# New issue order, PSUM banks and copy engines for a one-core attention and gated-MLP block

## The chip, the cores and the metric

The kernel runs on one core of one Trainium2 chip. The metric is device time in microseconds of one execution; the median of several runs is compared. A core has five instruction queues that run side by side: TensorE (PE, matrix products; its weight loads are shown as PEld), VectorE (DVE), ScalarE (ACT), GpSimd (POOL) and SyncE (SP), which here only issues DMAs. Each works its own list in order and waits on semaphores for the others.

## The reference: what is computed

One token block `x` of 2048 tokens by 448 columns goes through two stages, in bfloat16.

Stage A is attention with residual. `x` is normed per token (mean and variance over 448), multiplied by `wqkv` into q, k, v of 16 heads of 28 columns. Each token attends to itself and to seven earlier tokens at distance 2, 4, ... 14 (window 8, dilation 2); positions before the start are masked. The softmax-weighted sum of v is multiplied by `wo` and added to `x`: the result is `h`.

```python
off = jnp.arange(W) * dil            # W, dil = 8, 2
idx = pos[:, None] - off[None, :]
attn = softmax(where(idx >= 0, q . k[idx] * Dh ** -0.5, -1e9))
h = x + (attn . v[idx]) @ wo
z = gelu(layernorm(h) @ w_in)        # 448 -> 1792, z1 and z2 are its halves
g = einsum('ts,sf->tf', w_sp, layernorm(z2)) + b_sp[:, None]
h2 = h + (z1 * g) @ w_out
```

Stage B is a gated MLP. `h` is normed, multiplied by `w_in` (448 by 1792) and put through gelu. The second half of the columns, `z2`, is normed and mixed over all tokens by the 2048 by 2048 matrix `w_sp`; a bias per token is added, the first half `z1` is multiplied in, and `w_out` (896 by 448) brings it back to 448 columns, added to `h`.

## The kernel before

All work is cut into small jobs; each belongs to one engine and holds one or a few instructions. The names below are the job names in the code.

**Attention.** The 2048 tokens are 16 tiles of 128 (`NB`). Per tile m: statistics `st0_m`, mean and variance `mv0_m`, the inverse root `rs0_m` on GpSimd (for tiles 0 and 1 the epsilon is added on VectorE, `ra0_m`), the normed tile `n0_m`. It is transposed to `xhT`: the first four tiles by TensorE with an identity (`xTm`) and copies from PSUM (`xem_i`), the others by a transposing DMA, for which the last 64 columns are copied once more (`nd0_m`). The weights of q and k are padded by four copies `wpc`. Products `qk` (a first group of tokens 0 to 127, a second of 128 to 255 with jobs `qk0F0..2, qk0H, qk1F0..2, qk1H`, then `qk2` to `qk5`) are copied from PSUM by `qe`. The queries of even and odd tokens are handled apart in 17 blocks b (`GEOM`). For each block: two halves of the logits `lgb_0`, `lgb_1` on TensorE (`_0` on row tiles at 0 and 32, `_1` at 64 and 96), their exponentials `exb_0`, `exb_1` on ScalarE, one masking product `mkb` on VectorE, the product with the values and a column of ones `ob`, reciprocal `rcb` and multiplication `omb` on VectorE, the copy of the last columns `odb`, a transposing DMA `oTb`, and a gather `ocb` into `OT`. The values come in pairs of blocks (`vb`, copied by `veb`). For every two tiles, `ym` multiplies by `wo`, `hm` adds the residual on VectorE, and the second layer norm (`st1`, `mv1`, `rs1`, `n1`, `nd1`) ends in a transposing DMA `hTm`.

**MLP.** `z2_m` (16 products, one per tile) and `z1_u` (14 products of two PSUM banks) use `w_in`. Their gelus are on ScalarE (`z2gm`, `z1gu`); where `RAW2` says so, `z2` is first copied raw by `z2cm`. `st2`, `mv2`, `rs2` and `n2_m` norm `z2`. The mixing is cut into 28 tiles of 128 columns by 512 tokens; 13 pairs `gi` and two single ones `g26`, `g27`. Each pair is a list of 64-row products over the 16 tiles of `z2`, first all of kind `a` and then `b`; the first four pairs are cut in eight pieces `gi_0a` to `gi_7a`. VectorE adds the bias (`ua`) and multiplies with `z1` (`um`). `wom` are the output products of two tiles, `wpm_0` (and `_1`) those of the last four tiles one by one; `rm` adds the residual, `outm` stores.

**What sets the order.** Nothing is planned at run time. `Planner.job` lists 886 jobs, and `Planner.order` (line 284) only reads two tables: `ORDER` gives the sequence in which jobs are issued, each to its own engine's list, and `BANKS` the first PSUM bank of each of 147 tickets (a ticket is one or two of the eight banks of 512 columns that a TensorE job fills and another engine empties). `MODE` gives each product its form, in the function `product`. The contraction over 448 rows is three blocks of 128 rows and one of 64:

- `FH`: job `a` does the three blocks of 128 rows for both outputs (six matmuls), job `b` the 64-row rest, two matmuls side by side on the two 64-row tiles of the array.
- `HF`: the same, the rest first.
- `AB`: everything in 64-row halves, eight matmuls in `a` and six in `b`, in pairs side by side.
- `FF` (output products): all 128-row.

`ON` moves single copies to another engine than the default in `move`. Job 885 is a filler: one matmul of 256 columns on constants (line 1078), put where `ORDER` says. The other tables (`KEY`, `WLH`, `LN1G`) do not matter once `ORDER` is fixed.

**What makes a job wait.** `Sched.issue` (line 138) derives the waits from resources that jobs read and write. Each PSUM bank is such a resource (`r_bank`): a TensorE job writes all banks of its ticket, and a job that empties them reads them, so the next TensorE job on a bank waits for the readers of before (lines 1083 to 1094).

## Time and profile before

| what | value |
|---|---|
| runs | 243.03, 242.53, 243.61 us; median 243.03 |
| profiled execution | span 241.8 us, first to last instruction; the profile gives no other time of its own |
| granted TensorE clock, mean | 1.000 |
| instructions | 5654 |
| TensorE busy | 235.9 us, 2431 matmuls |
| VectorE, ScalarE, GpSimd busy | 149.3, 92.0, 40.0 us |
| DMA | 23.20 MB, 96 GB/s in the mean |

The span is shorter than the timed run, which also holds the start and the end of the program. Busy times are sums of durations on an engine. Matmuls overlap in the profile: one is listed with the time until its result is written, so the cost of a group of matmuls is read from its start to the next group's start. A line number such as L462 is that of the helper that issues the matmul of every product, so groups are told apart by the tiles they read (`xhT,wqk` is a `qk` product, `w_in,hnT` is `z1`, `hnT,w_in` is `z2`, `V,E` is `o`, `qkT` the logits, `warm` the filler). Idle time on an engine costs only if TensorE or the end waits for it.

### The profile page before, as it was taken

What the parts mean: (1) busy time and instruction counts of PE and PEld (TensorE: products, weight loads), DVE (VectorE), ACT (ScalarE), POOL (GpSimd) and SP (SyncE); (2) the same over time, 40 slices, a digit from 0 to 9 for tenths busy, and PEclk for the clock granted to TensorE, in tenths of its full rate; (3) what the DMA queues carried; (4) which work ended last, traced back from release to release, by engine and by line L of the source; (5) the groups of instructions that cost most, each with busy time, mean ns of one, the idle gap of its engine ahead of it and who ended that gap; (6) DMA issues with size and microseconds to landing.
All of it is one profiled execution on the core that took longest, in us unless ns stands there. A gap on an engine that the chain in (4) does not pass through costs nothing.

```text
span 241.8 us, 5654 instructions
## 1 busy us (share of the span) xinstructions
PE 235.9 (98%) x2431; PEld 116.3 (48%) x2431; DVE 149.3 (62%) x336; ACT 92.0 (38%) x109; POOL 40.0 (17%) x96
## 2 busy tenths in 40 slices
PE   6999999999999999999999999999999999999995
PEld 4774444554454544444444444444444444444453
DVE  5999988889999999998512306062029031301784
ACT  2478667888889958586802000000000000000000
POOL 6623410101354206235010100000000000000000
PEclk9999999999999999999999999999999999999999
DMA  6963546779698899979999000000000021000022
GB/s 176 308 162 58 115 91 89 158 156 185 129 141 146 129 189 163 221 155 168 191 177 204 3 0 3 0 3 0 0 3 1 0 79 38 0 3 0 3 94 95
DMA packets 66233, 23.20 MB, mean 96 GB/s; under 512 B 58656, under 2 KB 65952, under 8 KB 66208
## 3 DMA queue, kind: packets, MB, share of 16 engines
q1 hardware_dynamic: 66208, 22.83, 47.4%
q8 instruction: 19, 0.31, 0.5%
q14 instruction: 6, 0.05, 0.1%
HBM read 6.72 MB, written 1.84 MB: 35 GB/s over the span
## 4 chain that ended last, share of the span: by engine, by line
PE 88%; DVE 6%; ACT 2%; DMA 2%; issue 0%
PE psum L988 37%; PE psum L462 31%; PE psum L1036 7%; PE psum L1009 3%; PE psum L1078 3%; PE psum L1057 2%; DMA hnT<-xn 2%; PE psum L834 2%; PE psum L810 2%; DVE E L825 2%; ACT E L819 2%; PE psum L705 1%; DVE x_tm L775 1%; DVE st L621 1%; ACT V L505 1%; DVE xn L632 1%
## 5 line engine op out<-in xcount | busy, mean ns | idle before, releaser
L969 DVE TENSOR_TENSOR ub<-psum,bb 128x512 bf16<-128x512 f32 x28 | 18.1, 683 | 52.7 <-PE psum L988 52.7
L988 PE MATMUL psum<-wsp_hi,z2p 64*128 64x512 bf16 x384 | 42.1, 376 | 0.0
L819 ACT ACTIVATE E<-psum 128x960 bf16<-128x960 f32 (+2 forms) x34 | 31.6, 982 | 5.1 <-PE psum L810 4.9
L988 PEld LDWEIGHTS psum<-wsp_hi,z2p 64*128 64x128 bf16 x384 | 18.5, 94 | 23.0 <-issue 0.4
L988 PE MATMUL psum<-wsp_la,z2p 64*128 64x512 bf16 x224 | 26.6, 376 | 0.0
L988 PE MATMUL psum<-wsp_lb,z2p 64*128 64x512 bf16 x224 | 26.4, 376 | 0.0
L899 DVE BATCH_NORM_STATS2 st<-z2p 128x6 f32<-128x448 bf16 x32 | 18.8, 609 | 11.1 <-ACT z2p L895 8.4
L462 PE MATMUL psum<-w_in,hnT 64*128 64x448 bf16 (+1 forms) x206 | 24.9, 350 | 0.6 <-ACT E L819 0.3
L462 PE MATMUL psum<-xhT,wqk 64*128 64x512 bf16 (+3 forms) x206 | 24.4, 351 | 0.0
L462 PE MATMUL psum<-hnT,w_in 64*128 64x512 bf16 (+1 forms) x190 | 23.7, 376 | 0.0
L825 DVE TENSOR_TENSOR E<-E,maskb 128x1920 bf16<-128x1920 bf16 (+2 forms) x17 | 20.0, 1183 | 0.7 <-ACT E L819 0.6
L621 DVE BATCH_NORM_STATS2 st<-x_tm 128x6 f32<-128x448 bf16 x32 | 18.7, 608 | 1.7 <-DMA x_tm<-in_A_x_dram 1.6
L1017 DVE TENSOR_TENSOR srg<-psum,x_tm 128x448 bf16<-128x448 f32 (+1 forms) x17 | 9.5, 591 | 14.0 <-PE psum L1036 12.0
L612 POOL TENSOR_TENSOR rs<-rs,negh 128x2 f32<-128x2 f32 (+2 forms) x23 | 17.5, 759 | 3.4 <-DVE rs L611 1.6
L988 PEld LDWEIGHTS psum<-wsp_lb,z2p 64*128 64x128 bf16 x224 | 10.8, 94 | 13.4
L988 PEld LDWEIGHTS psum<-wsp_la,z2p 64*128 64x128 bf16 x224 | 10.8, 94 | 13.1 <-DVE ub L969 0.2
L1036 PE MATMUL psum<-w_out,z1p 128*128 128x448 bf16 x84 | 16.4, 353 | 0.0
L462 PEld LDWEIGHTS psum<-w_in,hnT 64*128 64x128 bf16 (+1 forms) x206 | 10.5, 94 | 11.8 <-issue 1.1
L937 ACT ACTIVATE z1p<-psum 128x1024 bf16<-128x1024 f32 x14 | 13.9, 1020 | 3.1 <-PE psum L462 2.9
L462 PEld LDWEIGHTS psum<-xhT,wqk 64*128 64x128 bf16 (+1 forms) x206 | 9.9, 94 | 9.8 <-issue 1.1
L462 PE MATMUL psum<-wv,xhT 64*128 64x448 bf16 (+1 forms) x86 | 14.2, 354 | 0.3 <-ACT V L505 0.2
L505 ACT ACTIVATE qkT<-psum 128x1024 bf16<-128x1024 f32 (+1 forms) x15 | 11.7, 828 | 7.2 <-PE psum L462 4.2
(69 smaller groups left out, 257.9 us busy)
## 6 DMA issues: line engine op xcount, KB each, us to landing
w_in<-in_B_w_in_dram SPq DMA_DIRECT2D x8, 224.0 KB, 3.5
out_dram<-srg SPq DMA_DIRECT2D x16, 112.0 KB, 1.7
x_tm<-in_A_x_dram SPq DMA_DIRECT2D x2, 448.0 KB, 5.3
w_out<-in_B_w_out_dram SPq DMA_DIRECT2D x1, 784.0 KB, 5.8
x_tm<-in_A_x_dram SPq DMA_DIRECT2D x3, 224.0 KB, 4.5
wq<-in_A_wqkv_dram SPq DMA_DIRECT2D x3, 224.0 KB, 3.9
bb<-in_B_b_sp_dram SPq DMA_DIRECT2D x1, 512.0 KB, 4.3
wo<-in_A_wo_dram SPq DMA_DIRECT2D x1, 336.0 KB, 5.8
```

The lines of the kernel that those rows point to most:

```text
L462: ins = e.matmul(o, w, x, start=k not in seen, stop=last, **kw)
L505: j = pl.job(name, eng, key, [(lambda e: e.activation(o(), i(), AF.Copy) if eng == "act" else e.tensor_copy(o(), i()), list(reads), list(w ...
L612: power = (lambda e: e.tensor_tensor(R, A, negh[:, 0:1].to_broadcast([128, n]), ALU.pow), [rr, r_negh], r_rs[k][m:m + n])
L621: [(lambda e: e.bn_stats(st[:, m, :], src), [rsrc], [r_st[k][m]])], dve_t(D))
L819: return e.activation(o, i, AF.Exp, scale=SCALE)
L825: return e.tensor_tensor(a, a, maskb[:, mi:mi + 1, pad:pad + nq].to_broadcast([NK, NHEAD, nq]), ALU.mult)
L899: [(lambda e, m=m, k=k: e.bn_stats(st3[:, m, k, :], z2p[:, m, D * k:D * (k + 1)]), [r_z2[m]], [r_st[2][m]])], dve_t(D))
L937: return e.activation(o, i, AF.Gelu_apprx_tanh)
L969: [(lambda e: e.tensor_tensor(ub[:, s, :], psv(tk, k), bb[:, 512 * tc:512 * tc + 512], ALU.add), [r_bb], [r_ub[s]])], dve_t(512), use=[tk] ...
L988: ins = e.matmul(psv(tk, k), z2p[h, s, 128 * fc:128 * fc + 128], wsp(s, tc)[h], start=n == 0 and s == 0, stop=n == len(lots) - 1 and s == ...
L1017: [(lambda e: e.tensor_tensor(srg[:, s, c0:c1], psv(tk, k, c1 - c0), x_tm[:, m, c0:c1], ALU.add), [r_x[m]], r_srg[2 * s + (c0 > 0):2 * s + ...
L1036: ins = e.matmul(psv(tk, k, D), z1p[h, fc, 128 * (m + k):128 * (m + k) + 128], w_out[h, fc, :], start=fc == 0 and (which == 0 or not half) ...
```

## The change

Four tables are replaced, and two places in the code.

- `ORDER`: another sequence of the same 886 jobs; the filler (885) stands in it 17 times and no longer 32.
- `BANKS`: other PSUM banks for the tickets; the filler's bank is 7, it was 0.
- `MODE`: of the 16 `qk` products 8 are `AB` (13 before), of 9 `v` products 4 (3), of 8 `y` products 4 (6), of 14 `z1` 12 (13), of 16 `z2` 14 (13); the others are `FH` or `HF`. The output products `wo` stay `FF`.
- `ON`: 54 copies change their engine. From ScalarE to VectorE 7, from VectorE to ScalarE 12, from GpSimd to VectorE 15, from VectorE to GpSimd 15, from ScalarE to GpSimd 4, from GpSimd to ScalarE 1.
- The last tile's output product is split at column 320 and no longer at 224.
- A job that gives back only a part of its ticket now waits for, and is waited for on, that part's banks alone.

The table `ORDER`, spelled out by names, for TensorE's list up to the first 30 jobs after the fillers:

```
before: 22 fillers, xT1, 6 fillers, xT0, 3 fillers, qk1F0 qk1F1 xT2 xT3 qk1F2 qk0F0 qk0F1 qk0F2 qk0H
        qk2_2a qk1H, filler, qk2_2b qk2_1a qk2_0a qk2_1b qk2_0b qk2_3a lg0_0 lg0_1 qk2_3b v0a v0b
        lg1_0 v2a lg3_0 lg3_1 v2b o0 v4a v4b lg2_0 qk3_1a qk3_0a o3 ...
after:  14 fillers, xT0, 3 fillers, xT1 qk0F0 qk1F0 xT2 xT3 qk0F1 qk1F1 qk1F2 qk0F2 qk1H qk2_0a
        qk0H qk2_0b qk2_2a qk2_3a qk2_2b qk2_3b qk2_1a lg0_0 lg0_1 qk2_1b v2a v2b lg3_1 lg2_0
        v0a v0b qk3_1a lg2_1 lg1_0 qk3_1b o0 qk3_3a lg3_0 lg1_1 ...
```

and for its end:

```
before: ... g9_0a g26_0 wo0a wo2a wo2b wo0b g27_0 wo6a wo6b g12_0a g9_1b g12_1b g10_0a g11_0a g10_1b
        g11_1b wo10a wo10b wo4a wo4b wo8a wo8b wp12_0 wp13_0 wp12_1 wp13_1 wp14_0 wp15_0 wp15_0
after:  ... g12_0a g11_1b g9_1b g12_1b wo0a wo2a wo0b wo4a wo4b wo6a wo2b wo8a wo8b wo6b wo10a wo10b
        g26_0 g27_0 wp13_0 wp12_0 wp12_1 wp13_1 wp15_0 wp15_0 wp14_0
```

VectorE's list begins, without the fill of `otm`, which moves behind the weight copies:

```
before: wset st0_1 st0_0 mv0_1 mv0_0 ra0_1 st0_3 st0_2 ra0_0 n0_1 mv0_2 wp0 mv0_3 n0_0 xe1_0 st0_4 n0_2 ...
after:  wset st0_0 mv0_0 ra0_0 st0_1 mv0_1 n0_0 ra0_1 st0_2 st0_3 n0_1 mv0_3 mv0_2 xe0_0 st0_5 st0_4 n0_2 ...
```

The diff, the long tables cut:

```diff
-MODE = {'qk2_0': 'AB', 'qk2_1': 'AB', 'qk2_2': 'AB', 'qk2_3': 'FH', 'qk3_0': 'AB', 'qk3_1': 'AB', 'qk3_2': 'AB',
...
+MODE = {'qk2_0': 'AB', 'qk2_2': 'AB', 'qk2_3': 'AB', 'qk2_1': 'AB', 'v2': 'HF', 'v0': 'FH', 'qk3_1': 'HF', 'qk3_3':
...
-ORDER = [6, 29, 33, 26, 134, 0, 34, 7, 885, 27, 885, 1, 885, 885, 31, 2, 885, 885, 885, 52, 11, 885, 42, 885, 32, 3,
...
+ORDER = [27, 0, 26, 134, 6, 42, 28, 7, 885, 885, 1, 885, 885, 11, 885, 44, 885, 2, 885, 885, 45, 885, 3, 46, 52, 885,
...
-BANKS = [2, 1, 1, 6, 2, 4, 2, 0, 6, 6, 0, 2, 2, 0, 0, 4, 6, 2, 4, 6, 6, 0, 2, 4, 0, 4, 4, 4, 7, 0, 6, 6, 6, 6, 0, 2,
...
+BANKS = [0, 2, 0, 1, 4, 6, 2, 4, 0, 6, 0, 6, 2, 4, 6, 4, 2, 0, 4, 6, 6, 0, 0, 2, 0, 0, 4, 0, 4, 6, 6, 4, 2, 0, 6, 2,
...
-ON = {'xe0_1': 'act', 'xe1_0': 'dve', 'xe2_0': 'dve', 'xe3_0': 'dve', 'nd0_6': 'dve', 'nd0_8': 'dve', 'nd0_10': 'dve',
...
+ON = {'wp0': 'act', 'xe0_1': 'act', 'xe0_0': 'dve', 'wp1': 'act', 'wp3': 'act', 'nd0_5': 'dve', 'nd0_4': 'dve',
+        'qe0_1': 'dve', 'nd0_6': 'dve', 'qe2_1': 'dve', 've2': 'dve', 'nd0_10': 'dve', 'od1': 'dve', 'od3': 'dve',
...
@@ -1048,7 +1046,7 @@
         def out_one(m, key):
             tc = m // 4
-            for c0, c1 in ([(0, D)] if m < NB - 1 else [(0, D // 2), (D // 2, D)]):
+            for c0, c1 in ([(0, D)] if m < NB - 1 else [(0, 320), (320, D)]):
                 tk = pl.ticket(1)
@@ -1083,7 +1081,8 @@
         for j in ordered:
             brs = []
             for t in j.tick:
-                brs += r_bank[t.b:t.b + t.n]
+                k, n = j.rel[1:] if j.rel is not None and j.rel[0] is t else (0, t.n)
+                brs += r_bank[t.b + k:t.b + k + n]
```

## The prediction

> **What bounds the kernel now.** I read the page's busy shares first, then who waits for whom on TensorE, then TensorE's instructions in order of time, then the other engines stage by stage.

> ```profile
> span 241.8 us, 5654 instructions
> ...
> PE 235.9 (98%) x2431; PEld 116.3 (48%) x2431; DVE 149.3 (62%) x336; ACT 92.0 (38%) x109; POOL 40.0 (17%) x96
> ```

> TensorE is busy for 98% of the span, so the time is the sum of what TensorE's list costs, item by item, plus what stands before its first useful item and after its last. Two kinds of its time are no arithmetic. The first is a change of row tiling. Some groups use all 128 rows (mode F of a product, the E·V products `o`, the transposes `xT`), some use two tiles of 64 rows (H, all of mode AB), and the logits `lg` use tiles of 32. Rows of the timeline of TensorE (start, duration, group):

> ```profile
> 34.20 1.89 PE L462 MATMUL psum<-xhT,wqk 64*128 64x512 bf16 x16
> 36.02 0.42 PE L810 MATMUL psum<-qkT 28*128 28x120 bf16 x16
> ...
> 40.41 1.03 PE L462 MATMUL psum<-xhT,wqk 64*128 64x512 bf16 x8
> 41.27 0.73 PE L462 MATMUL psum<-wo,OT 64*128 64x448 bf16 x6
> ```

> From 40.41 eight half matmuls take 0.86 us up to the next start, and the next group is of the same tiling. From 34.20 sixteen take 1.82 us, 0.10 more than twice 0.86, and a group of another tiling follows. I take 0.10 us for each change. The logits show something else as well, here in the chain of waits (start, length):

> ```profile
> 36.09 0.35 PE psum L810 x16
> ...
> 43.66 0.33 PE psum L810 x8
> ```

> Two groups of eight that lie side by side on different row tiles take 0.35 us together; one alone takes 0.33, with its change. A pair therefore saves about 0.2 us beyond the change that it also saves.

> The second kind is waiting. By starts, `o0` takes 0.69 us and `o2` 0.96 where an `o` takes 0.41, and the sixteen from 75.55 take 2.90 where their modes come to 2.47:

> ```profile
> 20.98 0.56 PE L834 MATMUL psum<-V,E 128*128 128x29 bf16 x16
> 21.67 1.61 PE L462 MATMUL psum<-wv,xhT 128*128 128x448 bf16 x8
> ...
> 30.95 0.56 PE L834 MATMUL psum<-V,E 128*128 128x29 bf16 x16
> 31.91 0.56 PE L834 MATMUL psum<-V,E 128*128 128x29 bf16 x16 [0.40 <-DVE E L825]
> ...
> 75.55 2.64 PE L462 MATMUL psum<-hnT,w_in 128*128 128x512 bf16 x16
> 78.45 0.37 PE L462 MATMUL psum<-w_in,hnT 64*128 64x448 bf16 x2 [0.26 <-DMA hnT<-xn]
> 78.75 0.56 PE L834 MATMUL psum<-V,E 128*128 128x29 bf16 x16
> 79.16 1.30 PE L462 MATMUL psum<-w_in,hnT 128*128 128x448 bf16 x6
> ```

> The last two rows give the plain `o`, 0.41 from start to start. Together that is 0.28 + 0.55 + 0.43, and with the others (0.4 at the most) about 2.0 us. All lie before 80 us; from there on nothing stalls TensorE. What feeds it is nearly as full (columns: window, length, PE, PEld, DVE, ACT, POOL busy, clock, DMA):

> ```profile
> 12.00:116.00 104.00, 102.72 (x1316) 51.73 (x1314) 96.91 (x222) 82.14 (x97) 30.39 (x64) 1.00 0.80 145
> 64.00:80.00 16.00, 15.41 (x217) 7.81 (x216) 15.54 (x33) 15.20 (x20) 7.64 (x14) 1.00 0.81 133
> ```

> VectorE works 96.9 of the 104 us from 12 to 116. It is the second bound, and it decides whether a shorter TensorE list can be used.

> **The change, part by part.** *Row changes.* I walked both issue lists by name, with both mode tables, and wrote down the tiling of each TensorE group. Without the fillers the tiling changes 74 times before and 52 times after (products of another kind are put between fewer logits, and F halves now stand next to `o` and to each other). 22 × 0.10 = 2.2 us less. Of the logits, 10 pairs and 14 singles become 14 pairs and 6 singles: 4 × 0.2 = 0.8 us less. The columns streamed are the same. These 3.0 us lie on the bounding engine; the list itself fixes them, and the row durations vary by hundredths.

> *Start.* The fillers go from 32 to 17, but they stand where TensorE has nothing else, so only the useful work's start counts. The chain of waits and the first rows of the other engines:

> ```profile
> 1.92 4.87 PE psum L1078 x22
> ...
> 8.77 0.43 PE psum L1078 x3
> ```
> ```profile
> 2.82 1.15 DVE L621 BATCH_NORM_STATS2 st<-x_tm 128x6 f32<-128x448 bf16 x2 [0.96 <-DMA x_tm<-in_A_x_dram]
> ...
> 6.04 0.39 DVE L632 TENSOR_SCALAR xn<-x_tm,mv,rs 128x448 bf16<-128x448 bf16 x1
> ```
> ```profile
> 4.40 0.57 POOL L612 TENSOR_TENSOR rs<-rs,negh 128x1 f32<-128x1 f32 x1 [0.66 <-DVE rs L611]
> ```
> ```profile
> 6.58 0.95 ACT L505 ACTIVATE wqk<-wq 128x896 bf16<-128x896 bf16 x1 [3.53 <-DMA wq<-in_A_wqkv_dram]
> ```

> Now the first norm waits behind the statistics of two later tiles and runs at 6.04. In the new VectorE order tile 0 has its statistics (2.82 to 3.43), mean and epsilon (to 3.85), then tile 1's statistics (to 4.6), then at once the norm, since GpSimd's power (0.57) is done by 4.6: 4.65 to 5.05. `xT0` can run at 5.1, `xT1` at 6.75, where they ran at 8.26 and 6.58. The last two norms move little (about 9.0 and 9.6, behind two statistics and the copy of half of tile 0), so `xT2` and `xT3` end near 10.15. ScalarE takes five of the first copies from VectorE and gives up two; its second weight copy, now behind one more x load, ends near 9.5, still before 10.15. From there TensorE has four 128-row products of 0.45 and one half product and is through with them at about 12.35. Before, the same set is done at 13.71, with 0.67 us more (`qk0H`, `qk2_2a`) and one filler (0.2) behind: 0.9 us gained. Bounds: 0 (the norms leave at the old pace) and 1.3.

> *Stalls.* I followed VectorE's, ScalarE's and SyncE's new queues at the durations of before to the instruction that each TensorE group reads or whose bank it reuses. The wait that comes out clearly is `lg3_1`, behind the VectorE copy `qe2_1` (14.9 us of VectorE work stand up to it, at the start's lag 18.0; TensorE is there at 17.6): 0.5. `v2a` waits 0.3 for a bank that ScalarE empties, and in the tail `wp12_0` waits 0.2. Many others arrive within half a microsecond (`o12`, `o16`, `lg5_0`, `z1_1a`), so I take 1.5 in place of 2.0: 0.5 gained. Bounds: 0.4 left (1.6 gained) and 4.7 (2.7 lost, the first rival).

> *Copies moved between engines.* 27 leave VectorE, 22 come to it. By such rows as these (median of a gather into OT 0.73, 0.43 or 1.21 on ScalarE, VectorE, GpSimd; 1.2 for a qk copy on VectorE) VectorE loses about 4.7 us, ScalarE gains 3.8, GpSimd 6.0:

> ```profile
> L505 ACT ACTIVATE OT<-OTs x7: 347/734/784, 43.6 to 89.7; 128x480 bf16<-128x480 bf16 x6, 128x96 bf16<-128x96 bf16 x1
> ...
> L505 DVE COPY OT<-OTs x6: 425/428/482, 38.4 to 89.5; 128x480 bf16<-128x480 bf16 x4, 128x512 bf16<-128x512 bf16 x1, 128x384 bf16<-128x384 bf16 x1
> L505 DVE CAST qkT<-psum x5: 691/1225/1225, 17.3 to 52.9; 128x1024 bf16<-128x1024 f32 x4, 128x512 bf16<-128x512 f32 x1
> L505 POOL COPY OT<-OTs x5: 623/1213/1658, 29.0 to 76.1; 128x480 bf16<-128x480 bf16 x2, 128x512 bf16<-128x512 bf16 x1, 128x96 bf16<-128x96 bf16 x1, 128x384 bf16<-128x384 bf16 x1
> ```

> So VectorE needs about 92 us where TensorE needs some 100: the cover holds, at nothing. If it did not, each microsecond of VectorE would be one of the kernel.

> *Waits by single bank* touch only copies that release one bank of two; TensorE still needs both of a pair, and after 80 us it waits for none. Nothing; bounds 0 and 0.2 gained. *SyncE's order* brings all but the first of the layer-norm transposes forward against the spatial weights, which now arrive last. By the walk through its queue the last of them, `wlo12` and `whi12`, land near 125 and 135 and are first read near 133 and 146. Nothing.

> *End.* The 320/128 split takes the same 448 columns, and tile 15 is no longer last; tile 14 is, whole. Its addition takes 0.62 in place of 0.39, bare on the path: +0.2 (bounds 0.1 and 0.4).

> ```profile
> 239.17 0.39 DVE L1017 TENSOR_TENSOR srg<-psum,x_tm 128x224 bf16<-128x224 f32 x1 [0.28 <-PE psum L1057]
> ```

> *Sum.* 241.8 − 2.2 − 0.8 − 0.9 − 0.5 + 0.2 = 237.6 us of span. The runs' median of 243.03 lies 1.2 above this span; the profile gives no other time of its own execution, so I carry 1.2 over: 238.8.

> **The rivals.** *VectorE sets the pace* (15 in 100). Laid on the pace at which VectorE got through its work before, the mask products of `o12`, `o14`, `o16` end 2.0 to 2.4 us, and the transpose for `z1_4` 2.7 us, after TensorE wants them. For it speaks 15.54 busy of 16 us; against it, that the old pace holds waits on TensorE that come earlier now. It decides if VectorE stays above 97% from 40 to 80. Then stalls are 4.7: 240.8 span, 242.0.

> *The fast clock comes late* (9 in 100). The fillers' rows show it: 22 in 4.87 us, 0.22 each, but 3 in 0.43 at 8.77, 0.14 each with what follows; TensorE doubled its speed near 8 us. After the change it idles from 4.4 to 5.1 and again near 6.6. If the doubling came only later, all from `xT2` to 12.35, 3 us of work, could take twice as long. Between none and 3.0 I take half, since part lies behind the norms: 1.5, so 240.3. [...]

> *GpSimd holds VectorE* (7, the slower side). GpSimd now has 12 of the OT gathers where it had 5, and its queue puts the powers of the second norm, `rs1_0`, `rs1_2` and `rs1_6`, behind `oc4`, `oc6`, `oc10`, which wait for a transpose to land. VectorE is in order, so `n1_0` would hold back every mask product behind it.

> ```profile
> POOL OT L505 <- DMA OTs<-otm: 8.6, 3, 4.1
> ```

> Such a wait is up to 4.1 us. By my walk `rs1_2` is ready as VectorE arrives, at 59. If the three come 2 to 4 us late each, the loss is about 7 us: 246. It decides from about 1.5 us late each.

> *Freed time is filled by waits* (4): the row changes vanish, but TensorE stands in their place and all four gains come back: 243. That the tables do not do what they say has no place here, since they fix the order.

> **How the numbers follow.** My forecast has 65 in 100: 238.8, by itself 237.3 to 240.5. A change under 0.5%, 241.8 to 244.2, is about what a measurement cannot tell from none. Faster: all of the forecast, the late clock, and half of VectorE's pace: 0.82. Same: the rest of it and the filled waits: 0.11. Slower: GpSimd: 0.07. Range 237.0 to 242.0: from all start and stall gains to VectorE's pace; the rest is left out.

> **What would show it.** Right: the first `xT` near 5.1 and `lg0_0` near 15.4; the logits as fourteen pairs; the first gate group near 115 us, with only one half of a `z1` product left behind it; stalls before 80 us under 2 us; a last addition of 0.6. Wrong: TensorE idle on E from VectorE between 60 and 80, VectorE idle on `rs` from GpSimd, fillers at 0.21 after 8 us, or waits after 116 us.

## The result, and the profile after

The changed kernel takes 241.50 us, the median of 18 executions (239.76 to 242.78), against 243.05 (242.51 to 244.01) for the kernel before. The ratio is 0.993 with a 95% interval of 0.9909 to 0.9951. That is 1.55 us faster where the prediction had 4.2, outside the forecast's own range of 237.3 to 240.5 and inside the wide range. The executions lie over 3.0 us, twice as far apart as those of before. A ratio leaves out executions more than 1.5% above the fastest of their kernel; in this study that is one, of `e11_first_gap`.

The profiled execution took 239.89 us, with a span of 238.2, so it is one of the fastest of the 18. The difference of 1.7 us between time and span is nearly the same (1.7 to 1.9) in all executions of this study. The first lines of its page:

```profile
span 238.2 us, 5559 instructions
...
PE 230.2 (97%) x2374; PEld 123.9 (52%) x2380; DVE 145.7 (61%) x331; ACT 93.8 (39%) x111; POOL 47.2 (20%) x99
```

TensorE is busy 5.7 us less than before, but the span is only 3.6 shorter: 2.1 us more of it are gaps. About half a microsecond of these stands ahead of three groups for which the trace lists five matmuls where the kernel issues six, so it need not be idle time. Its instructions in order of time (start, duration, group, idle time before it) show the gaps at the start:

```profile
1.38 3.17 PE L1076 MATMUL psum<-warm 128*128 128x256 bf16 x14 [1.38 <-DVE warm L580]
5.05 0.50 PE L660 MATMUL psum<-ident,xn 128*128 128x128 bf16 x3 [0.51 <-DVE rs L609]
...
6.48 0.34 PE L660 MATMUL psum<-ident,xn 128*128 128x128 bf16 x3 [0.27 <-DVE xn L630]
...
7.82 1.05 PE L703 MATMUL psum<-xhT,wqk 128*128 128x128 bf16 x16 [0.83 <-ACT xhT L503]
...
11.91 0.60 PE L460 MATMUL psum<-xhT,wqk 64*128 64x256 bf16 x8
```

The start is as it was walked in the prediction: `xT0` at 5.05 (forecast 5.1), `xT1` at 6.48 (6.75), the first half products behind the qk set at 11.91 (12.35). But TensorE idles for 0.83 us between `xT1` and the first qk product, and for 0.51 and 0.27 behind the fillers. Two more rows of the same view show the waits that came after the start:

```profile
20.26 0.39 PE L460 MATMUL psum<-xhT,wqk 64*128 64x512 bf16 x2 [1.09 <-DVE st L619]
...
82.75 1.04 PE L460 MATMUL psum<-hnT,w_in 64*128 64x512 bf16 x8 [0.40 <-ACT z2p L503]
```

The first is `qk3_1a`, the second `z1_4a`. (In these rows `hnT,w_in` with 512 columns is a `z1` product and `w_in,hnT` with 448 a `z2` product; the section on the time before has these two names the wrong way round.) The other engines in the stretches that the prediction looked at (window, length, PE, PEld, DVE, ACT, POOL busy, clock, DMA):

```profile
12.00:116.00 104.00, 101.88 (x1293) 55.59 (x1294) 92.91 (x214) 85.29 (x99) 38.48 (x76) 1.00 0.75 135
64.00:80.00 16.00, 16.00 (x203) 8.87 (x203) 15.10 (x35) 13.19 (x16) 6.57 (x11) 1.00 0.75 137
```

VectorE works 92.9 us there, where about 92 were forecast and 96.9 stood before. The end of the chain of waits (start, length, what):

```profile
82.76 33.93 PE psum L460 x336
116.68 0.86 PE psum L986 x8
117.55 0.65 PE psum L460 x6
...
235.37 0.62 DVE srg L1015
```

From 82.76 on nothing stalls TensorE; one half of a `z1` product lies behind the first gate group, and the last addition takes 0.62, both as forecast. The group itself starts at 116.68, where the prediction had it near 115. So the profiled execution misses its forecast span of 237.6 by only 0.6. The larger part of the miss, 241.50 − 239.89 = 1.6 us, lies between this execution and the typical one.

### The profile page after: what moved, and what is told of

Same layout as the page of the kernel before. It is cut to its first block, busy times and chain, and to the rows that moved or that the text cites. A ratio compares the mean times of both kernels' runs of the same rounds, so it can differ in the third digit from the quotient of the medians.

```text
span 238.2 us, 5559 instructions
## 1 busy us (share of the span) xinstructions
PE 230.2 (97%) x2374; PEld 123.9 (52%) x2380; DVE 145.7 (61%) x331; ACT 93.8 (39%) x111; POOL 47.2 (20%) x99
## 4 chain that ended last, share of the span: by engine, by line
PE 90%; DVE 3%; DMA 3%; SPq 2%; issue 1%; ACT 0%
PE psum L986 38%; PE psum L460 34%; PE psum L1034 7%; PE psum L832 3%; PE psum L1007 3%; PE psum L808 3%; DMA x_tm<-in_A_x_dram 3%; PE psum L1055 2%; SPq L518 2%; DVE st L619 1%; DVE qkT L503 0%; DVE E L823 0%; DVE V L503 0%; ACT z2p L503 0%; DVE srg L1015 0%
## 5 line engine op out<-in xcount | busy, mean ns | idle before, releaser
L986 PEld LDWEIGHTS psum<-wsp_hi,z2p 64*128 64x128 bf16 x384 | 21.7, 94 | 19.7
L460 PE MATMUL psum<-xhT,wqk 64*128 64x512 bf16 (+2 forms) x171 | 23.5, 343 | 1.7 <-DVE st L619 1.1
L460 PE MATMUL psum<-hnT,w_in 64*128 64x512 bf16 (+1 forms) x184 | 24.4, 376 | 0.4 <-ACT z2p L503 0.4
L610 POOL TENSOR_TENSOR rs<-rs,negh 128x2 f32<-128x2 f32 (+2 forms) x23 | 18.3, 794 | 4.5 <-DVE rs L609 2.7
L986 PEld LDWEIGHTS psum<-wsp_la,z2p 64*128 64x128 bf16 x224 | 12.7, 94 | 11.5
L986 PEld LDWEIGHTS psum<-wsp_lb,z2p 64*128 64x128 bf16 x224 | 12.7, 94 | 11.5
L460 PEld LDWEIGHTS psum<-w_in,hnT 64*128 64x128 bf16 (+1 forms) x212 | 12.0, 94 | 9.5 <-ACT z2p L893 0.2
L460 PEld LDWEIGHTS psum<-hnT,w_in 64*128 64x128 bf16 (+1 forms) x184 | 10.2, 94 | 10.4 <-issue 1.3
L503 ACT ACTIVATE qkT<-psum 128x1024 bf16<-128x1024 f32 (+1 forms) x16 | 13.3, 867 | 4.0 <-PE psum L460 2.7
L1015 DVE TENSOR_TENSOR srg<-psum,x_tm 128x448 bf16<-128x448 f32 (+2 forms) x17 | 9.4, 592 | 8.2 <-PE psum L1034 4.1
```

What stands on the lines that cost most here:

```text
L460: ins = e.matmul(o, w, x, start=k not in seen, stop=last, **kw)
L503: j = pl.job(name, eng, key, [(lambda e: e.activation(o(), i(), AF.Copy) if eng == "act" else e.tensor_copy(o(), i()), list(reads), list(w ...
L610: power = (lambda e: e.tensor_tensor(R, A, negh[:, 0:1].to_broadcast([128, n]), ALU.pow), [rr, r_negh], r_rs[k][m:m + n])
L986: ins = e.matmul(psv(tk, k), z2p[h, s, 128 * fc:128 * fc + 128], wsp(s, tc)[h], start=n == 0 and s == 0, stop=n == len(lots) - 1 and s == ...
L1015: [(lambda e: e.tensor_tensor(srg[:, s, c0:c1], psv(tk, k, c1 - c0), x_tm[:, m, c0:c1], ALU.add), [r_x[m]], r_srg[2 * s + (c0 > 0):2 * s + ...
```

## The experiments

Each kernel was timed beside the kernel before on the same chip, and its ratio is to that. A time in the text is the median.

### Which executions are long, and why: `e0_after`, `e1_more_fillers`, `e2_wlo6_later`, `e3_both`

The first two theories were that the clock of TensorE is lost in the start's gaps, and that SyncE's queue (a weight transpose ahead of the transpose of x tile 6) holds `qk3_1a`. The first kernel is the changed one without an edit.

> The changed kernel, unedited, for its spread and for a second profile. Theory C (clock): its executions differ by when TensorE's clock rises and whether it falls back once TensorE idles between the few fillers; executions with a lower mean granted clock (0.986, 0.993) are the longer ones, span 238 to 241 us, and in a profile of a longer execution the fillers or the first products run at half speed (0.21 us a filler, 0.87 us for a 128-row qk product of 0.45) after 6 us. Theory D (data): the clock is the same in all, and executions differ by when the first loads land; then the first transposes move and nothing runs at half speed.

The second puts fillers back into the gaps; the last PSUM bank, that of the fillers, is moved so that they wait for nobody (jobs 49, 57 and 139 are `xT0`, `xT1` and `qk0F0`):

```diff
+for job, n in ((49, 3), (57, 1), (139, 3)):      # ahead of xT0, xT1, qk0F0
+    ORDER[ORDER.index(job):ORDER.index(job)] = [885] * n
+BANKS[-1] = 3
```

> The changed kernel with 7 more fillers (3 before xT0, 1 before xT1, 3 before qk0F0, on a bank that is free until qk2_0a), so that TensorE has no gap from 1.4 to 8.3 us. Theory C: the clock rises at the latest near 8.4 us and does not fall back; median span falls by about 1.3 us, to 238.5 (240.2 us), and the spread from 3 us to about 1.5. Theory D: the same median (241.5) and spread, or up to 0.2 us worse.

The third issues the transposing load `wlo6` (job 698) later, the fourth has both edits:

```diff
+ORDER.remove(698)
+ORDER.insert(ORDER.index(88) + 1, 698)
```

> The changed kernel with one load of the spatial weights (wlo6) issued after the transposes xT5, xT4, xT7, xT6 and no longer ahead of them. Theory S (SyncE): in the profile after, wlo6 holds SyncE from 8.9 to 12.4 us, xT6 is issued at 17.3 and qk3_1 waits 1.26 us for it; without it that wait goes and the median falls by 0.8 to 1.2 us. Rival: qk3_1 waits for VectorE's copy ve2, which frees its banks (the profile names VectorE); then nothing changes (within 0.2 us).

> Both edits, the fillers and the later wlo6. If C and S both hold the gains add: 2.1 to 2.5 us below the changed kernel, about 239.2 us; if only one holds, that one's gain alone.

Measured: `e0_after` 241.3 (239.37 to 242.37, ratio 0.9916 [0.9885, 0.9946]); `e1_more_fillers` **239.63** (239.04 to 240.07, 0.9846 [0.9825, 0.9868]); `e2_wlo6_later` 242.16 (239.74 to 242.76, 0.9937 [0.9912, 0.9962]); `e3_both` 239.88 (239.33 to 240.57, 0.9864 [0.9843, 0.9886]). Seven fillers, which compute nothing, gain 1.7 us and bring the spread from 3.0 to 1.0. It is the clock. (The fillers don't close all gaps: in the profile of `e1_more_fillers` 0.28 us ahead of `xT1` and 0.54 ahead of the first qk product remain.)

```profile
6.41 0.34 PE L663 MATMUL psum<-ident,xn 128*128 128x128 bf16 x3 [0.28 <-DVE xn L633]
...
7.90 1.05 PE L706 MATMUL psum<-xhT,wqk 128*128 128x128 bf16 x16 [0.54 <-ACT xhT L506]
```

The profiled execution of `e0_after` (241.01 us, clock 0.993) shows how, first in stretches (the eighth number is the granted clock):

```profile
4.20:7.61 3.41, 1.71 (x15) 0.77 (x13) 3.38 (x12) 2.46 (x4) 1.79 (x4) 1.00 0.94 272
7.61:11.02 3.41, 3.21 (x28) 2.62 (x29) 3.32 (x12) 2.12 (x6) 1.73 (x5) 0.50 1.03 299
```

then in TensorE's instructions:

```profile
7.80 1.86 PE L703 MATMUL psum<-xhT,wqk 128*128 128x128 bf16 x16 [0.81 <-ACT xhT L503]
...
10.85 2.36 PE L703 MATMUL psum<-xhT,wqk 128*128 128x128 bf16 x40
```

The clock was up from 4.20 to 7.61, fell to half for exactly the next 3.41 us, and came back. In the falling stretch the sixteen qk products take 1.86 us, where the profiled execution of the changed kernel has 1.05 for the same sixteen. TensorE had been busy for 1.71 us of the 3.41 before. Other executions lose the clock by its late rise. That of `e2_wlo6_later` (242.09 us), in stretches of 3.41 us counted back from its first record of the clock:

```profile
2.39:5.80 3.41, 2.94 (x17) 1.69 (x15) 2.85 (x9) 0.64 (x1) 1.12 (x2) 1.00 0.89 234
5.80:9.21 3.41, 2.77 (x22) 1.96 (x22) 3.32 (x13) 3.27 (x6) 1.38 (x3) 1.00 0.98 297
9.21:12.63 3.42, 3.42 (x32) 2.79 (x30) 3.03 (x10) 1.66 (x3) 1.99 (x5) 1.00 1.10 337
```

The view prints 1.00 as long as the trace has no record of the clock; its first record here is the rise at 12.63, right after the first stretch without a gap. Before it the same sixteen qk products, at 7.82, take 1.86 us again. That stretches of this length also hold ahead of the first record is the author's reading. The rival, that the first loads land at other times, falls: `xT1` starts at 6.48, 6.47 and 6.43 in the profiles of the changed kernel, `e0_after` and `e2_wlo6_later`. Now the list of executions of the changed kernel can be read, 18 and 7 more in `e0_after`. Mean clocks of 0.993 and 0.986 are one and two stretches at half speed (0.5 × 3.41 of 240 us is 0.7%; the profiles of `e0_after` and, below, `e11_first_gap` show one and two): eight executions of the first kind lie at 240.7 to 241.4, two of the second at 242.6 and 242.7. With a mean of 1.0 there are four at 239.4 to 239.9, like the profiled one that rose at 5.60, and eleven at 241.5 to 242.8, like the one above that rose at 12.63; that these eleven rose late is inferred from this one profile. So only about one execution in six gets the clock early and keeps it.

The theory of SyncE falls. In `e2_wlo6_later` nothing is gained, and in `e3_both` SyncE is through with issuing `xT6`'s transfer 0.85 us earlier than in `e1_more_fillers` (11.96 + 5.17 = 17.13 for 11.64 + 6.34 = 17.98), but `qk3_1a`, which waits for it, starts only 0.29 earlier (19.62 for 19.91):

```profile
19.62 0.39 PE L465 MATMUL psum<-xhT,wqk 64*128 64x512 bf16 x2 [0.69 <-DMA xhT<-xn]
```

The wait is 0.69 us, against 0.85 in `e1_more_fillers`. Where the other half a microsecond goes was not followed further.

### The counter-test: gaps in the kernel before, `e4_before_thin`

```diff
+fillers = [i for i, job in enumerate(ORDER) if job == 885]
+for i in reversed(fillers[14:22] + fillers[22:26] + fillers[28:30]):
+    del ORDER[i]
```

> The kernel before with 18 fillers instead of 32: of the 22 ahead of xT1 the first 14 stay, of the 6 ahead of xT0 the last 2, of the 3 ahead of qk1F0 the last 1. Nothing else is touched, and no dense filler stood on the path: xT1 waits for the normalised rows until 6.58 us in any case. Theory of the clock (the gaps between fillers make the rise of TensorE's clock uncertain from one execution to the next): the median rises by 1 to 2 us, to 244.2 to 245.2, and the executions spread over 2.5 us or more where those of before spread over 1.5. Rival (fillers are only padding, the 14 at the beginning are enough, and after's spread comes from elsewhere in its order): the median stays within 0.3 us of before's 243.2, and the spread at 1.5.

244.91 us (244.08 to 245.36), ratio 1.0077 [1.0061, 1.0093]: 2.0 us slower than before for leaving out 14 instructions that compute nothing. The spread of 1.3 us did not widen as expected; all six executions lie above the longest of before (243.54). The stretches, up to the rise of the clock at 12.66:

```profile
5.83:9.24 3.41, 3.12 (x24) 2.31 (x25) 3.23 (x11) 1.96 (x3) 2.88 (x8) 1.00 0.97 311
9.24:12.66 3.42, 3.42 (x33) 2.79 (x31) 2.59 (x7) 0.49 (x2) 1.07 (x3) 1.00 1.02 310
```

and the same view of the kernel before, whose clock rises at 7.95:

```profile
4.54:7.95 3.41, 3.41 (x20) 2.23 (x19) 2.91 (x9) 0.95 (x1) 2.34 (x6) 1.00 0.94 273
```

Both rises come at the end of the first stretch in which TensorE is never idle. That fits the narrow spread of before. Its fillers and products leave no gap from 1.92 us on, so by an estimate from the 3.41 us a full stretch ends at 1.92 + 2 × 3.41 = 8.75 us at the latest, wherever the stretches happen to lie. The changed kernel's first run without a gap goes from 1.38 to 4.55, 3.2 us, and cannot fill a whole one.

### How much of the gap must be filled: `e11_first_gap`

```diff
+ORDER[ORDER.index(49):ORDER.index(49)] = [885] * 3     # ahead of xT0 alone
+BANKS[-1] = 3
```

> The changed kernel with 3 extra fillers, all ahead of xT0, in the gap from 4.3 to 5.0 us; the gaps of some 0.4 us ahead of xT1 and 0.5 to 0.8 us ahead of qk0F0 stay. The unedited kernel's record shows the granted clock fall to half for 3.41 us right after a stretch of 3.41 us (4.20 to 7.61) in which TensorE was busy 1.71 us. If the share of such a stretch decides: with 0.64 us more it is 2.35 of 3.41, and most of the gain of all 7 fillers comes, 239.6 to 240.2. If one gap of half a microsecond is enough to lose the clock: no gain, 241.3 with a spread of 2 us or more.

239.47 us, ratio 0.9856 [0.983, 0.9883]: three fillers in the right gap bring the median that seven bring. But they don't bring it every time: four of the six executions took 239.25 to 239.56, one 241.09 at a clock of 0.993, and one 243.03 at 0.986. That last one is the profiled one:

```profile
4.47:7.88 3.41, 1.90 (x17) 0.89 (x15) 3.38 (x12) 2.17 (x3) 1.65 (x4) 1.00 0.97 311
7.88:11.30 3.42, 2.94 (x26) 2.44 (x26) 3.33 (x12) 2.20 (x6) 1.56 (x4) 0.50 0.96 292
```

Again the clock falls after a stretch that was about half busy (1.90 of 3.41). That stretch holds 0.48 us of idle time ahead of `xT1` and 0.79 of the 1.27 us ahead of the first qk product. None of the six is of the kind that lies above 241.4 at a mean clock of 1.0, as eleven of 25 were. This fits a first gap that decides the rise and later ones that decide the fall, according to where the stretches lie; six executions and one profile don't prove it.

### The price of a row change: `e7_old_modes`, `e8_more_changes`

The first puts the old table of row modes on the new order, with the seven fillers:

```diff
+MODE = OLD_MODE        # the table of before, word for word
```

> The changed kernel with its 7 extra fillers (239.63 us) and the old table of row modes on the new order: 70 changes between half and full row tiling instead of 52, the same products. The prediction's term of 0.10 us per change: 18 x 0.10 = 1.8 us slower, 241.4, ratio near 0.992, all of it in busy time of TensorE between 10 and 116 us. Rival 1 (a change costs nothing that a neighbouring product does not hide): no difference, 239.6. Rival 2 (the modes matter by which bank they fill first, so by who waits on whom): the busy time is the same, and TensorE's idle time ahead of qk and z products grows by over 0.5 us.

246.02 us (245.88 to 246.16), ratio 1.0125 [1.011, 1.014]: 6.4 us slower than `e1_more_fillers`, far more than the 1.8 expected. The waits of TensorE in this kernel (line, what it waited for, us in total, times, longest) begin, behind the 1.4 us ahead of the first filler, with:

```profile
PE psum L473 <- DMA xhT<-xn: 0.8, 1, 0.8
PE psum L821 <- ACT z2p L516: 0.6, 1, 0.6
PE psum L473 <- ACT E L830: 0.5, 2, 0.3
PE psum L821 <- ACT qkT L516: 0.5, 1, 0.5
PE psum L845 <- ACT E L830: 0.5, 1, 0.5
```

Walked with the durations of the prediction, the list costs 1.8 us more; the other 4.6 stand at some twenty groups of 0.15 to 0.7 us that now wait for a copy or for E. The first row stands in `e1_more_fillers` as well. The busy sum, which the rival expected to stay, rises from 230.9 to 235.1; the author's reading is that a listed duration covers a short wait, as a logit pair of the changed kernel that came late is listed with 0.62 us and one that did not with 0.42 (41.90 and 45.31). The 4.6 are read from start to start. By this reading the rival of the waits holds for the larger part: a mode decides when each of the two banks is needed and given back, and the table is worth what it is worth only with its own order. This kernel can't price a change.

The second does, in a stretch without waits:

```diff
+for pair in ("z1_6 z2_0 z2_8 z1_3 z2_10 z1_8 z2_11 z2_9 z1_5 z1_9 z2_15 "
+             "z2_14 z1_10 z2_12 z2_13 z1_7 z1_13 z1_12 z1_11").split():
+    MODE[pair] = "FH"
```

> The changed kernel with its 7 extra fillers (239.6 us), in which the 19 pairs of z products from z1_6 to z1_11, between 90 and 118 us, run with one full-height bank ahead of one half-height bank (mode FH) in place of both in halves (AB): the same products, 70 changes of row tiling for 52, all of the 18 more in a stretch in which TensorE never waits. It measures the price of a change by itself. The prediction's 0.11 us a change in this stretch: 18 x 0.11 = 2.0 us, 241.6, and the first gate group starts 2.0 us later. Rival (a change is free and the old modes cost 6.4 us by waits alone): 239.6.

241.9 us (241.48 to 242.04), ratio 0.9943 [0.9927, 0.9958], 2.3 us over the 239.56 of `e10_pair_waits` below, which has the same modes as `e1_more_fillers` and ran on the same chip. The chain of waits of this kernel and, in the second fence, of `e10_pair_waits`:

```profile
82.62 36.27 PE psum L466 x226
118.89 0.86 PE psum L992 x8
119.97 88.92 PE psum L992 x824
```

```profile
82.20 33.93 PE psum L463 x336
116.13 0.86 PE psum L989 x8
...
117.64 88.92 PE psum L989 x824
```

From the first z product of the stretch to the long run of gate products it is 37.35 us against 35.44. In the two traces the tiling changes 70 and 52 times. The 1.91 us more are 18 changes, so **0.106 us each**, in a stretch where no product is late in either kernel. The prediction's 0.10 stands.

### The wait near 82 us: `e5_hT6_early`

The chain of waits of `e1_more_fillers` shows how hT6 comes late:

```profile
76.96 0.63 DVE otm L846
...
77.58 0.30 DVE xn L633
...
79.06 3.61 DMA hnT<-xn
82.81 33.93 PE psum L463 x336
```

The norm n1_6 stands on VectorE behind the last multiplication of the attention (`om16`, 76.96) and runs at 77.58; GpSimd then copies its last columns (0.23 us for that copy in the changed kernel), and the transpose is issued at 79.06 and read at 82.81. On top of the seven fillers:

```diff
+for job, ahead in ((373, 375), (374, 373), (377, 376)):   # n1_6, nd1_6, hT6
+    ORDER.remove(job)
+    ORDER.insert(ORDER.index(ahead) + 1, job)
```

> The changed kernel with its 7 extra fillers (as in e1_more_fillers, 239.63 us) and with three jobs moved ahead: n1_6 on VectorE right behind n1_7 and so ahead of the second head group's last rows, the copy nd1_6 right behind it, and the transposing transfer hT6 right behind nd1_7, ahead of oT15. Theory: the idle time of 0.8 to 0.9 us ahead of z1_4a near 82 us, which waits for hT6's landing, is on the path; hT6 then lands 1 us or more earlier, the wait goes, and the time falls by 0.6 to 0.9 us, to 238.8 to 239.0, ratio to before near 0.982. Rival: the wait only moves, because the rows of n1_6 then hold up the masking of the last rows and oT15 comes later, so that v16 or the z2 products near 68 us wait instead: TensorE's idle time between 60 and 100 us stays at 1 us, and the time at 239.6.

239.39 us (239.26 to 239.73), ratio 0.9856 [0.9843, 0.9869]: by the ratios no gain over `e1_more_fillers`. In the trace the transfer is issued 2.7 us earlier, at 76.36, but TensorE waits only 0.4 us less:

```profile
81.99 1.04 PE L466 MATMUL psum<-hnT,w_in 64*128 64x512 bf16 x8 [0.38 <-ACT z2p L509]
```

`z1_4a` waited 0.81 for the transfer in `e1_more_fillers`; now it waits 0.38 for ScalarE's copy of a z2 bank, which was late in any case. The rival was right that the wait moves, but not where: it went to the next in line at the same product, on ScalarE.

### The end, and the three together: `e6_narrow_tail`, `e9_best`

```diff
+TAIL = ORDER.index(874) + 1
+ORDER[TAIL:] = [875, 871, 877, 880, 872, 882, 876, 878, 879, 881, 883, 884]
+BANKS[-4] = 7
```

> The changed kernel with its 7 extra fillers (239.63 us) and another order of the last products: row block 14 in one piece ahead of row block 15, whose 320 columns come next and whose 128 columns come last; block 14 gets a PSUM bank of its own. Theory (TensorE ends when it ends, and what follows it is one addition): the last addition is 128 wide, 0.28 us instead of 0.62, and the time falls by 0.3 us, to 239.3, ratio near 0.983. Rival (the end is set by the last store, whose time from issue to landing does not depend on when the last addition ends, or by the store of row block 14 queued ahead of it): no change.

239.02 us (238.98 to 239.76), ratio 0.9846 [0.9832, 0.986], the same ratio as `e1_more_fillers`. The trace has the edit's effect: VectorE's last group, the second addition of which is 128 wide, starts at 234.38 and is through at 235.07, 0.34 us after TensorE's last product; in `e1_more_fillers` the addition alone takes 0.62.

```profile
233.43 0.62 DVE L1021 TENSOR_TENSOR srg<-psum,x_tm 128x448 bf16<-128x448 f32 x1 [0.17 <-PE psum L1061]
...
234.38 0.69 DVE L1021 TENSOR_TENSOR srg<-psum,x_tm 128x320 bf16<-128x320 f32 x2 [0.33 <-PE psum L1061]
```

A third of a microsecond is below what these ratios tell. `e9_best` has the fillers, the earlier hT6 and the narrow end.

> The changed kernel with the 7 extra fillers, the earlier hT6 and the narrow last piece together. If the three gains are apart from each other (start, wait near 82 us, end): 239.6 - 0.4 - 0.3 = 238.9, ratio near 0.982. If z1_4a goes on waiting for ScalarE's copy at 82.0 us whenever hT6 lands, hT6 gives nothing and the time is that of the narrow tail, 239.1.

239.28 us, ratio 0.9848 [0.9817, 0.988]; five executions at 238.71 to 239.70 and one at 241.20, which has no profile and a mean clock of 1.0. In all 37 executions of kernels with the seven fillers the mean clock is 0.999 or 1.000, so none lost the clock after its rise; whether the one at 241.20 got it late is not known. The profiled one of `e9_best` waits 0.46 us ahead of `z1_4a`, for ScalarE's copy again. The 238.9 is not excluded, nor is no gain at all: beside the fillers none of the edits can be told from nothing. `e1_more_fillers` is the plain version that beats both kernels, by 1.5% [1.3%, 1.8%] over before.

### Waits by pairs of banks: `e10_pair_waits`

```diff
-                k, n = j.rel[1:] if j.rel is not None and j.rel[0] is t else (0, t.n)
-                brs += r_bank[t.b + k:t.b + k + n]
+                brs += r_bank[t.b:t.b + t.n]
```

> The changed kernel with its 7 extra fillers (239.6 us) and the waits for PSUM by pairs of banks as before: a product waits for both banks of its pair, even where a reader uses one. The prediction put the single-bank waits at nothing: 239.6, within 0.3 us. Rival (the new order was made for them, and a first half that must wait for the second bank's copy stands 0.3 to 0.5 us at several pairs): 240.2 to 241.5, with new idle time ahead of qk and z products on the copies of ScalarE and VectorE.

239.56 us (239.44 to 240.07), ratio 0.9854 [0.9834, 0.9873], 0.07 us from `e1_more_fillers`. The finer waits do nothing here, as the prediction had it.

## Why the prediction was right and wrong, point by point

*The failed step is in the start: the prediction put the loss of 15 fillers at nothing, and the clock that they had held up among the rivals, at 9 in 100.* "The fillers stand where TensorE has nothing else, so only the useful work's start counts" was wrong: the fillers cost nothing, but their absence does, 1.7 us by the seven fillers put back and 2.0 by the 14 taken from the kernel before. The prediction saw the gaps from 4.4 to 5.1 and near 6.6, named the late clock and priced it at 1.5 us. That price was about right for the median (241.50 − 239.89 = 1.6 from the executions); the chance was not. The row that should have raised it was in its own quotation: 22 fillers in 4.87 us, in a kernel whose TensorE has no gap from 1.92 us on. After the change the first run without a gap is 3.2 us, shorter than the stretch of 3.41 us that, when full, was followed by the fast clock in each profile listed at the end. More than 1.5 was lost at times: the late rise in `e2_wlo6_later` goes with 242.09 us, 2.2 over the early one, and four executions at 242.6 to 242.8 lie 2.8 to 3.0 us over the fastest, two of them with a mean clock of 0.986, the value of the profile of `e11_first_gap`, in which the clock fell back at 7.88.

*Stalls* were sized at 1.5 us, and the profiled execution has about 2.5 behind the start, read from start to start as the prediction read its 2.0. None of the three that were named came: `lg3_1`, `v2a` and `wp12_0` follow the product before them at once. In their place stand `qk3_1a` (1.1 idle, 1.26 by starts), `z1_4a` (0.40 idle, 0.56 by starts; 0.81 idle in another execution) and five of the fourteen logit pairs, 0.6 together. `qk3_1a` starts 0.25 us after the transfer of x tile 6 lands (20.01), as in `e1_more_fillers` (19.66 and 19.91), so it waits for that and not for the VectorE instruction that its row names. Of the pairs, one that came late and one that runs side by side, each with the group behind it:

```profile
41.90 0.62 PE L808 MATMUL psum<-qkT 28*128 28x120 bf16 x16
42.45 0.56 PE L832 MATMUL psum<-V,E 128*128 128x29 bf16 x16
...
45.31 0.42 PE L808 MATMUL psum<-qkT 28*128 28x120 bf16 x16
45.66 0.56 PE L832 MATMUL psum<-V,E 128*128 128x29 bf16 x16
```

From start to start the first takes 0.55 us, the second 0.35; the five take 0.43 to 0.56. What held their second halves was not followed. The wait of `z1_4a` was in the prediction, but under the rival of VectorE's pace as a transfer 2.7 us late. +1.0 us.

*The start* came 0.4 us better than forecast where the clock was up in time: the qk set is through by 11.91, forecast 12.35.

*The 1.2 us carried over* from span to time should have been 1.7, as the executions now show with both numbers. The profiled execution of before was thus at 243.5, half a microsecond over its median, and the sum was set against the median. +0.5 us.

Together: 237.6 + 1.0 − 0.4 + 1.7 = 239.9, which is the profiled execution, and 1.6 for the typical one gives 241.5.

*Row changes* (−2.2): the price is confirmed by itself, 0.106 us. In the traces the tiling changes 72 times before and 50 times after between 13 and 122 us, 22 fewer as walked. That all 22 came back as time is not shown: it was not tested apart from the order, and `e7_old_modes` could not do it. *Logits* (−0.8): fourteen pairs, as forecast, but the five late ones give back 0.6 of it, which is counted under the stalls; not tested by itself. *Copies moved* (0): right, VectorE at 92.9 us (GpSimd gained 8.1 where 6.0 were forecast, ScalarE 3.2 where 3.8 were). *Single-bank waits* (0): right. *SyncE's order* (0): nothing waits for a weight behind 116 us; right. *End* (+0.2): right, 0.62 for 0.39.

*The other rivals.* VectorE does not set the pace: TensorE is busy for all 16 us from 64 to 80, VectorE for 15.1. GpSimd does not hold VectorE. Two rows of the changed kernel's waits:

```profile
DVE z2p L906 <- POOL rs L610: 2.7, 3, 1.1
...
DVE xn L630 <- POOL rs L610: 2.2, 3, 1.1
```

The longest such wait is 1.1 us, and TensorE was not late for one of them. The gains were not filled by waits, except for the 1.0 us above.

## What to carry to other kernels

Before you take out or space out instructions that only keep an engine busy, look at when the granted clock changes in the traces. Work out the longest run without a gap and compare it with the stretch that, when full, was followed by the fast clock, 3.41 us here; by an estimate from it a run of twice that, 6.8 us, holds a full stretch wherever the stretches lie. Price a change in the start over several executions, since one profile shows only one position of the stretches (the same kernel's clock rose at 5.60 in one and at 4.20 in another), and a profiled execution among the fastest hides the loss (239.89 us, with a median of 241.50). A table of modes that was made for one order could not be priced on another (by the reading above 4.6 of the 6.4 us of `e7_old_modes` are waits); vary it in a stretch where nothing waits, as `e8_more_changes` does.

## What the runs showed of the hardware

The clock rose after each of the seven stretches at half speed that were read as fully busy: in the kernel before (4.54 to 7.95), `e2_wlo6_later` (9.21 to 12.63), `e4_before_thin` (9.24 to 12.66), `e5_hT6_early` (2.20 to 5.62), `e8_more_changes` (3.92 to 7.34), `e9_best` (2.28 to 5.69) and `e11_first_gap` (11.30 to 14.71). After partly busy stretches it rose four times (2.82 and 3.21 us of the 3.41 in `e0_after`, 2.90 in the changed kernel, 3.09 in `e11_first_gap`) and did not rise after 2.94 in `e2_wlo6_later` and `e11_first_gap` or 3.12 in `e4_before_thin`. It fell after 1.71 (`e0_after`) and 1.90 (`e11_first_gap`), and at the end of the changed kernel (at 237.71) after 1.04, and not after 2.31 and 2.47 (the changed kernel from 5.60 to 9.02, `e9_best` from 5.69 to 9.10). So busy time alone doesn't order these cases; what decides after a partly filled stretch is not shown.

A transfer whose issue was through earlier was not read earlier by as much: 0.85 us on SyncE between `e1_more_fillers` and `e3_both` brought `qk3_1a`, which waits for `xT6`, forward by 0.29.
